# Two placements in a fused attention and long-convolution kernel: the sum of two spectra moved from VectorE to two transfers, and a table's index arithmetic moved behind two copies

## The chip, the cores and the metric

The kernel runs on one core of a Trainium2 chip. The metric is the time of one execution on the device, in microseconds; three runs of the kernel before gave 213.45, 213.49 and 214.47, so the median is 213.49. The engines are TensorE (PE in the profile, with its weight loads as PEld), VectorE (DVE), ScalarE (ACT), GpSimd (POOL) and SyncE (SP). SP, ACT and POOL also issue transfers, each on a queue of its own: q1 is SP's, q10 ACT's, q0 POOL's.

## The reference, cut to what matters

Two independent computations over a sequence of S = 2048 rows of D = 576 columns; their outputs are laid side by side.

```
a:  qkv = x @ wqkv                       # 32 heads of 18
    logits = q . k[s - 2*u], u = 0..7    # sliding window of 8, dilation 2
    attn = softmax(logits); o = sum_u attn * v[s - 2*u]
    a = o @ wo
b:  k_shift = 4-tap causal convolution of k with shift_k
    kv = k_shift * v
    y = causal convolution of kv with ssm_k (length 2048, by FFT) + kv * ssm_D
    b = q * y
out = concatenate([a, b])
```

## The kernel before, in words

**Part b** cuts the sequence into NBL = 4 blocks of BL = 512 rows. Each block of kv ("x" in the names) and each block of the filter is turned into a spectrum by matmuls with tables of sines: `x_spectrum(i)` (L759 to L770, tile `ps_fx`) and `filter_spectrum(m)` (L662). A spectrum has two parts of HB = 4 x 576 = 2304 columns, which ScalarE copies from PSUM to SBUF, x's to the tile `xw`, the filter's to `Ks`. The complex products are made with three multiplications instead of four, and for these each spectrum also needs a third part, the sum of the first two, kept 2 x HB columns behind the first. `XG` gives the place of each x spectrum in `xw`: block 3 has its parts at HB x 6, HB x 7 and HB x 8. HB x 8 is also where block 3 of kv itself lies until its spectrum is made.

Who makes a third part differs. For most, `produce` (L1237) puts an addition on VectorE (L1247) ahead of the first product that needs it. For those listed in the set `given`, `third` (L697) has made it by two transfers earlier: SP copies part 0 to the place of the third part (L700), and POOL adds part 1 to it with an accumulating transfer (`add_half`, L689), which waits for the copy. Before the change this is done for x's block 2 and the filter's block 2 (`third_x(2)`, `third_k(2)`, L1062 and L1063).

Output block j is the sum over i <= j of the products of x's block i with the filter's block j - i. `todo` (L1225) lists the 30 products in the order of (j, t, i), t being one of three thirds of the columns. VectorE makes each (`products`, L1092 to L1100, 128 x 2304 elements), TensorE adds them up in PSUM by matmuls with plus and minus the identity (`sum_of`, L1126, tile `ps_z`), ScalarE evicts the sums to `av` (L1139), TensorE turns them back with the table TI (`inverse`, L1158, tile `ps_inv`; the last piece at L1177) and mirrors them (`ps_back`, L1199 and L1185), ScalarE evicts again, and VectorE multiplies with q ("the gate": L1212 for blocks 0 to 2, L1167 for block 3). `load_q(j)` (L1085) brings the rows of q for this with three transfers on POOL's queue: blocks 0 and 1 ahead of the products, block j + 2 after the gate of block j. `store_b` writes the result.

**Part a** is projections (`ps_proj`), logits (VectorE products at L822, summed by head on TensorE in `ps_log`), a softmax, a weighing of v (VectorE products at L947, summed in `ps_acc`) and the output projection: `output` (L1003) makes one half (288 of 576 columns) of 128 rows of two sequence halves in a PSUM pair `ps_wo`, ScalarE evicts it to a staging tile (L1031), and after the second half ACT issues the store of the tile (L1035). The staging tiles are used in turn: a place in `qk`, one in `TB`, and a second one in `qk` that is dropped once the products of part b have begun. From then on an eviction into a staging tile waits for the store before last.

**Order.** The order of all work is fixed when the program is built. Units of TensorE work stand in one list, `units`; the stages pull them by counts written out by hand (`PLACES`, `FKS`, `FXS`) at calls of `until`, or by `need(label)`, which pulls all units up to the last one with that label. The units of part a's output projection that are left over are interleaved with the products of part b. The loop at the end produces the products up to three ahead of the sums. `ps_wo`, `ps_inv` and most others share two PSUM pairs with tag A, `ps_z` and `ps_acc` two with tag B.

**The start.** The tables are sines of integers. `table` (L419) computes the integers on VectorE into `n_all` with two multiply-adds (L421) and one masking (L422), and returns the function that later has ScalarE take the sines (L423). `table_k(0)` and `table_k(1)` serve the filter's spectra, `table_x(0)` and `table_x(1)` x's. Between them stand two copies of transposed rows of A_x from PSUM into `xT` on VectorE (L510, beside two on ScalarE, L511), which the first projections (`project_first`, L483) read. The list `sines` keeps the four functions in the order table_k(0), table_k(1), table_x(0), table_x(1); ScalarE calls them later in the order 2, 3, 0, 1.

Of the kernel before, what the change touches and what calls it, by code (L numbers as in the profile page):

```python
# [39 lines left out]
def view(t, offset, dims):  # L40

    return bass.AP(tensor=t.tensor, offset=t.offset + offset, ap=[list(t.ap[0])] + [list(d) for d in dims])
# [3 lines left out]
def kernel(  # L46
# [293 lines left out]
    def need(label):  # L340
        while any(u[2] == label for u in units):
            pop()
# [76 lines left out]
    def table(n_i, T, vec, cols, period, offs):  # L419
        for n in range(2):  # L420
            nc.vector.tensor_scalar(n_i[:, n, :], vec, rp[:, cols[n]:cols[n] + 1], offs[n], op0=ALU.mult, op1=ALU.add)  # L421
        nc.vector.tensor_single_scalar(n_i, n_i, period - 1, ALU.bitwise_and)  # L422
        return lambda: nc.scalar.activation(T, n_i, ACT.Sin, bias=pib[:], scale=-2.0 * np.pi / period)  # L423

    def table_k(c):
        return table(n_all[:, 2 * c:2 * c + 2, :], TK[:, c, :, :], n_all[:, 8, :], (2 + c, 2 + c), 2048, (256.0, 1792.0))

    def table_x(n):
        return table(n_all[:, 4 + 2 * n:6 + 2 * n, :], TX[:, 2 * n:2 * n + 2, :], n_all[:, 8, :], (4, 5), 4096,
              (512.0 + 1024.0 * n,) * 2)  # L430
# [31 lines left out]
    def pair_x():  # L462
        return pp.tile([128, 2, 1024], BF16, name="ps_x", tag="B")
# [13 lines left out]
    def project_first(jp, ct0):  # L477

        ps = bank2("ps_proj", "A")
        for e in range(2):  # L480
            c0 = 128 * (ct0 + e)
            for kb in range(4):
                nc.tensor.matmul(ps[:, e, :], wq(kb, 0, c0, 128), xT(kb, 512 * jp, 512), start=(kb == 0), stop=False)  # L483
        for e in range(2):
            nc.tensor.matmul(ps[:, e, :], wq(4, 0, 128 * (ct0 + e), 128)[64 * jp:64 * jp + 64],
                             x5(0)[64 * jp:64 * jp + 64], start=False, stop=True, tile_position=(64 * jp, 0))
        nc.scalar.activation(view(q, S * ct0 + 512 * jp, [[S, 2], [1, 512]]), ps[:], ACT.Copy)

    def spread_taps(n0):
        n = min(256, D - n0)  # L490
        ps = bank2("ps_sk", "A" if n == 256 else "B")
        for h in range(0, n, 128):
            w = min(128, n - h)
            sk = skrow[:, 4 * (n0 + h):4 * (n0 + h + w)].rearrange("p (d j) -> p d j", j=4)
            for r in range(2):
                nc.tensor.matmul(ps[:, h // 128, 0:4 * w], ones96[:, 128 * r:128 * r + 128],  # L496
                                 sk if r else view(skrow, 4 * (n0 + h) + 3, [[4, w], [-1, 4]]),
                                 start=(r == 0), stop=(r == 1))
        nc.scalar.activation(skb[:, :, n0:n0 + n],
                             ps[:].rearrange("p b (d j) -> p j (b d)", j=4)[:, :, 0:n], ACT.Copy)  # L500

    spread_taps(512)
    spread_taps(0)
    sines = [table_k(0), table_k(1)]
    pts = [pair_x() for _ in range(2)]
    for n in range(2):
        transpose_x(0, pts[n], 2 * n, range(4))
# [3 lines left out]
        nc.scalar.activation(xT(2 + n, 0, 512), pts[1][:, n, 0:512], ACT.Copy)  # L511
    copy_tail(0, pts[1])
    spread_taps(256)
    sines += [table_x(0), table_x(1)]
    project_first(0, 0)
    pts = [pair_x() for _ in range(2)]
    for n in range(2):
# [179 lines left out]
    def third(t, at):  # L697

        given.add((t is xw, at))
        nc.sync.dma_start(half(t, at + 2 * HB), half(t, at))  # L700
        add_half(t, at + 2 * HB, at + HB)

    def third_x(i):
        need(f"fx{i}")
        third(xw, HB * XG[i])
# [366 lines left out]
    def upper(t, j, a, width, c0, n):  # L1072

        return bass.AP(tensor=t.tensor, offset=t.offset + (BL * j + 320 - 64 * a) * width + c0,
                       ap=[[width, 64], [(64, 192)[a] * width, 2], [1, n]])
# [9 lines left out]
    def load_q(j):  # L1085
        qB = view(TB, HB * (j % 2), [[D, 4], [1, D]])
        nc.gpsimd.dma_start(qB[:, 0:2], qf[BL * j:BL * j + 256, :].rearrange("(c p) d -> p c d", c=2))  # L1087
        for a in range(2):
            nc.gpsimd.dma_start(qB[64 * a:64 * a + 64, 2:4], upper(qf, j, a, D, 0, D))
        qBs[j] = qB  # L1090
# [134 lines left out]
    todo = [(j, t, i) for j in range(NBL) for t in range(3) for i in range(j + 1)]  # L1225
    load_q(0)
    load_q(1)
    clk["P"] = clk["D"]
    groups = []
    for n, (j, t, i) in enumerate(todo):  # L1230
# [73 lines left out]
```

## Time and profile before

| | us |
|---|---|
| median of three runs | 213.49 |
| the profiled execution, its time | 213.4 |
| the profiled execution, its span | 211.7 |
| TensorE busy in the span | 200.2 |
| VectorE busy | 197.5 |
| ScalarE busy | 150.7 |
| GpSimd busy | 71.5 |

The profile is of one execution. All times within it count from the start of the span; the time of an execution is somewhat longer than the span, here by 1.7 us. A row of a timeline gives the start, the duration of the merged instructions, the engine, the line of the kernel, the operation, "out<-in" with the tiles' names, the shape, the count, and in brackets the idle time of the engine just before and what ended it. A row of the table by stretches gives, for each engine, the busy time within the stretch and the count of instructions, and after them the granted TensorE clock (1.00 is full), the mean busy share of the 16 DMA engines, and what they moved in GB/s. A row of DMA issues gives the tiles, the issuing engine, the count, the size of one, and the median time from issue to landing; a row of a DMA queue gives its packets, the MB moved, and the time of its packets as a share of 16 engines over the stretch asked for.

### The profile page before, as it was taken

To read this page: it belongs to the slowest core of one execution; us is meant where nothing else is said; L and a number is where in the kernel's file an instruction comes from. 1 tells how busy PE (TensorE), PEld (TensorE's weight loads), DVE (VectorE), ACT (ScalarE), POOL (GpSimd) and SP (SyncE) were. 2 spreads that over 40 slices of the span, in tenths; PEclk is the share of its full clock that TensorE was granted. 3 is DMA by queue.
4 is the path that set the end of the run, shared out by engine and by line. 5 is a ranking of instruction groups with operands and counts; after the bars stand their busy time and mean duration, and the time that the engine had idled before them with its cause. 6 is when DMAs were issued, how large, how long until landed. Compare 5 with 4: busy or idle time off the path is not lost.

```text
span 211.7 us, 5087 instructions
## 1 busy us (share of the span) xinstructions
PE 200.2 (95%) x2114; PEld 113.1 (53%) x2122; DVE 197.5 (93%) x150; ACT 150.7 (71%) x218; POOL 71.5 (34%) x104
## 2 busy tenths in 40 slices
PE   7999899999879999999999999999999999999891
PEld 3543344444545556563345556765566667676560
DVE  7999999999978999979979999999999999899982
ACT  3699766967796989984378678864487897765640
POOL 8999995021591467220090000004240000302000
PEclk9999999999999999999999999999999999999999
DMA  6999999999193636999999797598993105453034
GB/s 205 302 337 225 267 329 301 189 282 190 35 127 41 87 54 102 186 160 181 228 241 225 133 220 167 101 211 249 209 278 109 60 3 158 124 167 115 3 105 118
DMA packets 34084, 36.12 MB, mean 171 GB/s; under 512 B 17459, under 2 KB 28847, under 8 KB 34062
## 3 DMA queue, kind: packets, MB, share of 16 engines
q1 hardware_dynamic: 26380, 23.11, 44.2%
q0 software_dynamic: 5216, 10.19, 24.7%
q10 hardware_dynamic: 2466, 2.51, 3.6%
q8 instruction: 16, 0.26, 0.5%
q14 instruction: 6, 0.05, 0.1%
HBM read 13.11 MB, written 4.72 MB: 84 GB/s over the span
## 4 chain that ended last, share of the span: by engine, by line
PE 83%; ACT 10%; issue 3%; DVE 2%; DVEq 0%; ACTq 0%
PE ps_proj L363 15%; PE ps_z L1126 9%; PE ps_wo L1020 8%; PE ps_acc L964 7%; PE ps_inv L1158 7%; PE ps_fx L766 7%; PE ps_log L837 4%; PE ps_proj L483 3%; PE ps_fk L610 3%; ACT Ks L670 3%; PE ps_proj L374 3%; PE ps_proj L367 3%; PE ps_rev L650 1%; PE ps_sk L496 1%; ACT qk L397 1%
## 5 line engine op out<-in xcount | busy, mean ns | idle before, releaser
L363 PE MATMUL ps_proj<-xw 128*128 128x512 bf16 x153 | 36.2, 380 | 1.3 <-issue 0.6
L822 DVE TENSOR_TENSOR av<-qk 128x4096 bf16<-128x4096 bf16 (+1 forms) x16 | 31.5, 2018 | 2.3 <-ACT xw L592 2.3
L363 PEld LDWEIGHTS <-xw 128*128 128x128 bf16 x160 | 14.4, 98 | 20.0 <-issue 4.9
L1139 ACT ACTIVATE av<-ps_z 128x768 bf16<-128x768 f32 x23 | 17.4, 809 | 5.5 <-PE ps_z L1126 5.5
L768 ACT ACTIVATE xw<-ps_fx 128x576 bf16<-128x576 f32 x32 | 18.8, 670 | 2.4 <-PE ps_fx L766 2.4
L397 ACT ACTIVATE qk<-ps_proj 128x1024 bf16<-128x1024 f32 x14 | 14.3, 1023 | 8.3 <-PE ps_proj L374 4.7
L670 ACT ACTIVATE Ks<-ps_fk 128x576 bf16<-128x576 f32 x32 | 18.9, 683 | 1.1 <-PE ps_fk L611 1.0
L1098 DVE TENSOR_TENSOR qk<-xw,Ks 128x2304 bf16<-128x2304 bf16 x14 | 18.6, 1354 | 1.0 <-PE ps_z L1126 0.7
L560 DVE TENSOR_TENSOR tB<-kj,skb 128x4608 bf16<-128x4608 bf16 (+1 forms) x8 | 19.4, 2431 | 0.1
L766 PE MATMUL ps_fx<-xw,TB 128*128 128x288 bf16 x128 | 17.9, 286 | 0.8 <-ACT xw L592 0.7
L1020 PE MATMUL ps_wo<-qk 128*128 128x288 bf16 x128 | 18.0, 287 | 0.0
L610 PE MATMUL ps_fk<-Ks,TB 128*128 128x384 bf16 x62 | 16.4, 326 | 1.2 <-ACT Ks L670 0.9
L1158 PE MATMUL ps_inv<-av,TI 128*128 128x288 bf16 (+1 forms) x112 | 15.6, 292 | 0.6 <-ACT av L1139 0.6
L766 PEld LDWEIGHTS <-TB 128*128 128x128 bf16 x128 | 12.0, 98 | 6.7 <-issue 3.5
L1087 POOL DMA_DIRECT2D TB<-in_B_q_dram x4 | 2.9, 736 | 36.7 <-DVE v L1098 23.6
L964 PE MATMUL ps_acc<-av,ident 64*64 64x512 bf16 x160 | 15.3, 379 | 0.0
L611 PE MATMUL ps_fk<-Ks,TB 128*128 128x192 bf16 x62 | 15.2, 246 | 0.0
L397 ACT ACTIVATE v<-ps_proj 128x1024 bf16<-128x1024 f32 x9 | 9.3, 1040 | 7.8 <-PE ps_proj L363 4.3
L1020 PEld LDWEIGHTS <-qk 128*128 128x128 bf16 x128 | 11.5, 98 | 6.3 <-issue 3.6
L968 ACT ACTIVATE qk<-ps_acc 128x1024 bf16<-128x1024 f32 x8 | 8.2, 1024 | 8.3 <-PE ps_acc L964 8.3
L947 DVE TENSOR_TENSOR av<-Ks,v 128x4096 bf16<-128x4096 bf16 x6 | 13.6, 2286 | 0.1
L1158 PEld LDWEIGHTS <-TI 128*128 128x128 bf16 x112 | 10.5, 98 | 5.6 <-issue 2.7
(194 smaller groups left out, 468.2 us busy)
## 6 DMA issues: line engine op xcount, KB each, us to landing
Ks<-Ks POOLq DMA_DIRECT2D x7, 576.0 KB, 8.5
TB<-av SPq DMA_DIRECT2D x12, 256.0 KB, 5.5
kj<-in_B_k_dram SPq DMA_DIRECT2D x6, 504.0 KB, 5.8
vt<-in_B_v_dram SPq DMA_DIRECT2D x8, 288.0 KB, 4.9
Ks<-av SPq DMA_DIRECT2D x8, 256.0 KB, 5.7
out_dram<-qk ACTq DMA_DIRECT2D x5, 288.0 KB, 3.2
Ks<-in_A_x_dram SPq DMA_DIRECT2D x2, 576.0 KB, 5.1
xw<-in_A_wqkv_dram SPq DMA_DIRECT2D x2, 576.0 KB, 5.8
```

The lines of the kernel that those rows point to most:

```text
L363: nc.tensor.matmul(ps[:, jp, :], wq(kb, comp, 128 * ct, 128), xT(kb, 1024 * jj + 512 * jp, 512), **se)
L397: nc.scalar.activation(view(t, o + pad + 1024 * jj, [[512, 2], [1, 512]]), ps[:], ACT.Copy)
L560: dve(2304 * n, lambda: nc.vector.tensor_tensor(to, view(kj, row * D, [[D, n], [D, 4], [1, D]]), view(skb, row * D, [[D, n], [0, 4], [1, D ...
L610: nc.tensor.matmul(o[:, 0:2], w, rhs[:, 0:2], start=start, stop=stop)
L670: nc.scalar.activation(view(Ks, k_at(m, cs ^ (m & 1)) + 96 * gi, [[768, 3], [384, 2], [1, 96]]), acc3(ps), ACT.Copy, scale=(PSG, MSG)[cs][ ...
L766: nc.tensor.matmul(ps[:, pm, 0:HD], TX[:, 2 * pm + c, 128 * gi:128 * gi + 128], kv[:, 2 * c + pm, HD * h:HD * h + HD], start=(c == 0), sto ...
L768: nc.scalar.activation(view(xw, HB * XG[i] + 96 * gi + 1152 * h, [[HB, 2], [384, 3], [1, 96]]), view(ps, 0, [[512, 2], [96, 3], [1, 96]]), ...
L822: return P, at, step, dve(1024 * nj, lambda: nc.vector.tensor_tensor(view(P, at, [[step, 4], [256, nj], [1, 256]]), view(t, o + 256 * hh, ...
L964: nc.tensor.matmul(acc[64 * o:64 * o + 64, h, :], ident[64 * h:64 * h + 64, 64 * h:64 * h + 64], view(P, 256 * u, [[2048, 2], [1, 256]])[6 ...
L1020: nc.tensor.matmul(ps[:, r, 0:HD], oT(hh, j + 2 * r, t)[:, o:o + 128], wo[:, t // 2, t % 2, HD * h:HD * h + HD], start=(t == 0 and h == 0) ...
L1126: nc.tensor.matmul(view(acc[r], 512 * h, [[192, 2], [96, 2], [1, 96]])[o:o + 64], w[64 * h:64 * h + 64, 64 * h:64 * h + 64], pr[64 * h:64 ...
L1158: nc.tensor.matmul(ps[:, c, 0:n], TI[:, sl, pm, 128 * c:128 * c + 128], Yall[:, j % 2, pm, sl, c0:c0 + n], start=(pm == 0 and sl == 0), st ...
```

## The change

Three edits, two of which belong together:

```diff
     spread_taps(512)
     spread_taps(0)
-    sines = [table_k(0), table_k(1)]
+    sines = [table_k(0)]
     pts = [pair_x() for _ in range(2)]
...
     copy_tail(0, pts[1])
     spread_taps(256)
-    sines += [table_x(0), table_x(1)]
+    sines += [table_k(1), table_x(0), table_x(1)]
     project_first(0, 0)
...
     load_q(0)
     load_q(1)
+    third_x(3)
     clk["P"] = clk["D"]
```

The first two move the index arithmetic of `table_k(1)` on VectorE from ahead of the two copies of L510 to behind them. The order of the four functions in `sines` stays, and with it the order on ScalarE.

The third lists block 3 of x in `given`, so `produce` no longer puts VectorE's addition of 128 x 2304 elements ahead of the product (j, t, i) = (3, 0, 3). In its place `third` issues two transfers of 128 x 2304 elements within `xw`: a plain one on SP's queue, behind the third part of the filter's block 2, and an adding one on POOL's queue, behind the six transfers of q for blocks 0 and 1. The functions that it calls are as they were:

```python
    def add_half(t, to, of):
        nc.gpsimd.dma_start(half(t, to), half(t, of), accum_op=ALU.add, max_dma_last_dim=HB)
...
    def third(t, at):
        given.add((t is xw, at))
        nc.sync.dma_start(half(t, at + 2 * HB), half(t, at))
        add_half(t, at + 2 * HB, at + HB)
...
    def third_x(i):
        need(f"fx{i}")
        third(xw, HB * XG[i])
```

The order of the instructions on TensorE and ScalarE is the same in both kernels. VectorE has one instruction less and the two copies earlier; SP and POOL have one transfer more each.

## Prediction
> **What bounds the kernel now.** I read the page's totals and chain first, then the table of busy time by stretches for the end, then timelines of single engines around the two places that the change touches, and last the DMA views around the new transfers.
>
> ```profile
> span 211.7 us, 5087 instructions
> PE 200.2 (95%) x2114; PEld 113.1 (53%) x2122; DVE 197.5 (93%) x150; ACT 150.7 (71%) x218; POOL 71.5 (34%) x104
> ...
> PE 83%; ACT 10%; issue 3%; DVE 2%; DVEq 0%; ACTq 0%
> ...
> 185.00:190.00 5.00, 5.00 (x73) 3.48 (x72) 5.00 (x5) 2.72 (x5) 0.00 (x0) 1.00 0.52 168
> 190.00:195.00 5.00, 5.00 (x88) 3.27 (x90) 4.90 (x5) 2.91 (x5) 1.92 (x3) 1.00 0.42 130
> ```
>
> TensorE and VectorE are both nearly always busy, and the totals do not say which one sets the end. The chain does: 83% of it is TensorE, 2% VectorE. In the end stage (columns: stretch, its length, then busy time of PE, PEld, DVE, ACT and POOL, granted clock, DMA share, GB/s) both are full from 185 to 195, TensorE at full clock. What matters is which of them waits for the other there.
>
> ```profile
> 189.18 1.35 DVE L1247 TENSOR_TENSOR xw<-xw 128x2304 bf16<-128x2304 bf16 x1
> 190.63 1.36 DVE L1098 TENSOR_TENSOR qk<-xw,Ks 128x2304 bf16<-128x2304 bf16 x1
> 194.44 2.62 DVE L1098 TENSOR_TENSOR qk<-xw,Ks 128x2304 bf16<-128x2304 bf16 x2
> 202.06 1.35 DVE L1212 TENSOR_TENSOR TB<-v,TB 128x2304 bf16<-128x2304 bf16 x1
> 204.31 0.96 DVE L1137 CAST av<-ps_z 128x768 bf16<-128x768 f32 x1 [0.90 <-PE ps_z L1126]
> ...
> 197.13 0.35 PE L1126 MATMUL ps_z<-qk,ident 64*64 64x384 bf16 x4
> ...
> 198.55 1.46 PE L1158 MATMUL ps_inv<-av,TI 128*128 128x384 bf16 x8 [0.58 <-ACT av L1139]
> ```
>
> VectorE's last products end at 202.06 (it starts the gate there) and it then stands 0.90 us until TensorE has made the sum that it casts. TensorE's only sizeable gap, 0.58 us, is ScalarE's eviction of a sum that TensorE itself had just finished. So at the end TensorE leads and VectorE follows.
>
> **The change part by part.** *The removed VectorE addition.* It is the row at 189.18; the next instruction starts at 190.63, so 1.45 us of VectorE time go. The products behind it come up to 1.45 us earlier. The tightest of them is the second of the pair at 194.44: it ends at 194.44 + 2.62 = 197.06, and TensorE takes it up at 197.13, 0.07 us later, with no idle time printed before it. All that follows on VectorE ends in the wait of 0.90 us, which becomes about 2.35. I put the gain at 0. The bounds are 0 and 1.45 us, the latter if TensorE were in truth waiting at 197.13. The cover is TensorE's own row of work; with that gone, the whole 1.45 would be gained.
>
> *The table's index arithmetic.*
>
> ```profile
> 5.09 1.80 PE L450 MATMUL ps_x<-ident,Ks 128*128 128x128 bf16 x16
> 5.66 0.93 DVE L421 TENSOR_SCALAR Ks<-Ks,rp 128x512 int32<-128x512 int32 x2
> 7.16 1.04 PE L496 MATMUL ps_sk<-tB,ones 97*128 97x512 bf16 x4
> 7.24 0.75 DVE L510 COPY xw<-ps_x 128x512 bf16<-128x512 bf16 x2
> 8.03 1.89 PE L483 MATMUL ps_proj<-xw 128*128 128x512 bf16 x8
> 11.56 1.36 DVE L560 TENSOR_TENSOR xw<-kj,skb 128x2304 bf16<-128x2304 bf16 x1 [0.42 <-ACT qk L487]
> ```
>
> The two copies move ahead of one table (three instructions, 5.66 to 7.24). Their source, the first eight transposes, is there at about 5.09 + 1.80/2 = 6.0, so they start about 1.2 us earlier. TensorE reads them in L483 at 8.03, but it is busy with L496 from 7.16 until then: gain 0. VectorE would stand for about 6.0 - 5.7 = 0.3 us ahead of the copies, and the last table ends that much later; the 0.42 us idle ahead of L560 take it. Without that cover it would cost 0.3 us. I take 0, bounds -0.1 to +0.3.
>
> *The two new transfers.* The plain one goes on SP behind the third of Ks (SP row at 142.41 below) and needs only the last spectrum's evictions, which are over by then, so it starts near 143. The adding one goes on POOL behind the six transfers of q, the last of them issued by 154.82 + 1.24 = 156.06, and takes some 1.2 us to issue: traffic from about 157.5. Behind it on POOL stand only the next rows of q at 179.61. SP's next issue is at 176.80. So neither queue is held up. Its reader, the product at 190.63, comes some 25 us after any landing seen (at most 8.5 us); that wait costs nothing.
>
> ```profile
> 142.41 0.52 SPq L700 DMA_DIRECT2D Ks<-Ks  x1
> ...
> 176.80 0.42 SPq L1080 DMA_DIRECT2D out_dram<-TB  x1
> ...
> 146.19 1.18 POOL L689 DMA_DIRECT2D Ks<-Ks  x1 [0.75 <-issue]
> ...
> 154.82 1.24 POOL L1089 DMA_DIRECT2D TB<-in_B_q_dram  x2
> 179.61 0.73 POOL L1087 DMA_DIRECT2D TB<-in_B_q_dram  x1 [23.55 <-DVE v L1098]
> ...
> Ks<-Ks POOLq DMA_DIRECT2D x1, 576.0 KB, 8.5
> ```
>
> What they do cost is room on the DMA engines, and there one transfer is already waited for:
>
> ```profile
> 157.56 0.38 ACTq L1035 DMA_DIRECT2D out_dram<-qk  x1
> ...
> 162.08 0.65 ACT L1031 ACTIVATE qk<-ps_wo 128x576 bf16<-128x576 f32 x1 [1.44 <-DMA out_dram<-qk]
> 162.62 1.51 ACT L1139 ACTIVATE av<-ps_z 128x768 bf16<-128x768 f32 x2
> ...
> out_dram<-qk ACTq DMA_DIRECT2D x1, 288.0 KB, 4.4
> ...
> 161.75 2.17 PE L1020 MATMUL ps_wo<-qk 128*128 128x288 bf16 x16
> 163.99 0.33 PE L1126 MATMUL ps_z<-qk,identn 64*64 64x384 bf16 x4
> ```
>
> The store issued at 157.56 lands 4.4 us later, at 161.96, and ScalarE, which fills the same staging rows again, stands 1.44 us for it until 162.08. Behind that eviction on ScalarE's queue are the two evictions of sums at 162.62. TensorE's next output unit, the second half of the row at 161.75 (from about 162.84), needs the PSUM pair that the waiting eviction frees at 162.08 + 0.65 = 162.73. The slack is 0.1 us: any later landing goes nearly whole into TensorE, and there is no later gap that takes it back. So the price of the change is how much later this store lands.
>
> ```profile
> 147.61 0.38 ACTq L1035 DMA_DIRECT2D out_dram<-TB  x1
> ...
> out_dram<-TB ACTq DMA_DIRECT2D x1, 288.0 KB, 7.2
> ...
> 160.66 0.38 ACTq L1035 DMA_DIRECT2D out_dram<-TB  x1
> ...
> out_dram<-TB ACTq DMA_DIRECT2D x1, 288.0 KB, 2.2
> ...
> q0 software_dynamic: 234, 0.50, 86.8%
> q10 hardware_dynamic: 147, 0.17, 18.3%
> ...
> q10 hardware_dynamic: 255, 0.28, 30.6%
> ...
> 156.00:158.00 2.00, 2.00 (x26) 1.44 (x28) 1.90 (x4) 1.53 (x3) 0.06 (x1) 1.00 1.02 265
> 158.00:160.00 2.00, 2.00 (x31) 1.40 (x24) 1.91 (x3) 1.96 (x4) 0.00 (x0) 1.00 0.75 219
> 160.00:162.00 2.00, 2.00 (x33) 1.22 (x32) 2.00 (x2) 0.64 (x2) 0.00 (x0) 1.00 0.26 90
> ```
>
> A store of the same size landed in 2.2 us with the engines free (issued at 160.66), in 4.4 us beside the tail of q, and in 7.2 us where two adding transfers were under way (issued at 147.61). The rows of q0 and q10 with 86.8% and 18.3% are of 148.8 to 152.0, beside those adds; 30.6% is q10 in 157.5 to 160.2, nearly all of the store in question. In the former, the adds moved 0.50 MB in 0.868 x 3.2 = 2.78 us of all engines, so 0.59 MB of one add need some 3.3 us. The DMA share is 1.02 until 158 and falls after it, and into that fall the add is put: its 3.3 us lie right beside the store. The plain copy lands its own load on an interval (143 to 147) from which the engines are full up to 158, and so pushes the rows of q back by its size, bounded by 0 and by the cost of an add, 3.3 us.
>
> Bounds for the store's landing: 4.4 us (no effect) and 7.2 us (wholly beside adds), with some delay of q's tail on top, at most 9. As its first microsecond still runs beside q as before and the rest beside the add, I take two thirds of the way from 4.4 to 7.2, or 6.3 us: landing at 163.9, 1.9 us later, less 0.1 us slack is 1.8 us. The second store (160.66) is then late too, but the eviction that waits for it stands on ScalarE's queue behind the delayed ones and moves with them. Sum: 0 + 0 + 1.8. The profiled execution took 213.4 us (span 211.7 and 1.7 around it; the median of the runs is 213.49): 213.4 + 1.8 = 215.2 us.
>
> **The rivals.** *The store takes turns evenly with the add.* From the rows above a packet of an add takes 0.868 x 3.2 x 16 / 234 = 0.19 us on its engine, one of a store 0.183 x 3.2 x 16 / 147 = 0.064 us; a store has 255/16 = 16 for each engine. Alone they need 1.0 of the 2.2 us, so 1.2 us are fixed. One for one with the add: 1.2 + 16 x 0.254 = 5.3 us, a landing 0.9 us later, +0.8: 214.2 us. Against it: in 148.8 to 152.0 there went 234 packets of the add to 147 of the store, 1.6 to one, at which the store takes 1.2 + 16 x 3.2 / (147/16) = 6.8 us, or +2.3 (215.7). The Trainium skill ("DMA: Bandwidth & Descriptors", section "Queues, rings and completion order") states the even turn, each DMA engine going round its queue rows packet by packet; by that rule the sum would be 214.2, and the trace agrees only in part, with 1.6 to one.
>
> *The transfers are hidden anyway.* If POOL issues the add later than I count, or the store's data is through before the add's begins, nothing moves: 213.4. For it: the DMA share is down to 0.26 from 160 on, so most of the store's bytes had gone by then. Against: a share of 1.02 just before.
>
> *Faster: VectorE did set TensorE's pace.* The 0.07 us at 197.13 say that the product arrived just in time; if the weight loads ahead of it had been held back, TensorE's stretch from 190 on would shrink with VectorE. It decides from the point at which a product is later than TensorE's own readiness, and gives at most 1.45: 212.0, likelier half of it, 212.7. Against it stand 5.00 us of TensorE in each of the two stretches from 185 to 195, and the first gap after them waits for ScalarE.
>
> *Worse: both adverse bounds meet*, q pushed back and the store starved until the add is done, landing 8.7 us after issue: 166.3, +4.1, 217.5.
>
> **How the numbers follow.** Forecast case (delay of 1.1 to 3 us) 0.47; the worse case 0.08; even turns 0.22; hidden 0.13; faster 0.10. Own range of the forecast: 214.5 to 216.4. A measurement of this kernel tells about 0.5% (1.07 us) from no change. Slower by more: 0.47 + 0.08 = 0.55. Even turns, hidden and the smaller half of the faster case lie within it: about 0.38. Faster by over 0.5%: 0.07. The range leaves out the upper part of the worse case and the full gain: 213.0 to 217.0.
>
> **What would show it.** ScalarE's wait for the store ahead of L1031 at 162.08 should grow from 1.44 to about 3.3 us, the store's landing from 4.4 to about 6.3, and an idle stretch of about 1.8 us should appear on TensorE ahead of an L1020 near 162.8. The adding transfer should issue near 156 and land before 168. From 190 on VectorE should wait longer for TensorE, the 0.90 us ahead of the cast growing to some 2.3. At the start L483 should still begin at 8.0 and L560 at 11.6. I am wrong if the landing stays below 5 us (no change), if the end stage from 185 to the end shrinks by over 0.5 us (VectorE led), or if a wait for the added transfer shows up ahead of the product that reads it.

## The result and the profile after

| | before | after |
|---|---|---|
| median, us | 213.47 (213.36 to 214.47, 4 runs) | 220.63 (218.37 to 221.70, 4 runs) |
| the profiled execution, its time | 213.4 | 221.7 |
| its span | 211.7 | 220.0 |

The ratio of the times is 1.0293, 95% interval 1.0243 to 1.0344: the change makes the kernel about 6 us slower. The ratio leaves out executions that took over 1.5% longer than the fastest of the same kernel, here the profiled one of the changed kernel, while the medians are of all. The place is the one that the prediction named, the size is not. The timeline of ScalarE in the kernel after, with the stores that ACT issues:

```profile
159.06 0.38 ACTq L1035 DMA_DIRECT2D out_dram<-qk  x1
...
168.65 0.65 ACT L1031 ACTIVATE qk<-ps_wo 128x576 bf16<-128x576 f32 x1 [6.50 <-DMA out_dram<-qk]
```

The same wait was 1.44 us before. TensorE's timeline behind it:

```profile
163.26 1.15 PE L1020 MATMUL ps_wo<-qk 128*128 128x288 bf16 x8
169.35 1.94 PE L1020 MATMUL ps_wo<-qk 128*128 128x288 bf16 x8 [4.93 <-ACT qk L1031]
...
173.59 2.13 PE L1158 MATMUL ps_inv<-av,TI 128*128 128x288 bf16 x16
```

Before, both output units stood in one row without a gap (161.75, 2.17 us for 16), and the inverse followed 2.56 us after the start of the second (162.84):

```profile
165.40 2.13 PE L1158 MATMUL ps_inv<-av,TI 128*128 128x288 bf16 x16
```

Now 4.93 us lie between them, and the second, the same eight matmuls, takes 1.94 us in place of 1.15. The table by stretches says why (the last three columns are the granted clock, the DMA share and GB/s):

```profile
170.00:171.00 1.00, 1.00 (x6) 0.49 (x4) 0.00 (x0) 1.00 (x2) 0.00 (x0) 0.50 0.00 0
...
172.00:173.00 1.00, 1.00 (x16) 0.54 (x12) 0.00 (x0) 0.41 (x1) 0.00 (x0) 0.53 0.88 308
173.00:174.00 1.00, 1.00 (x20) 0.56 (x13) 0.98 (x1) 0.61 (x1) 0.00 (x0) 1.00 0.01 3
```

After the idle stretch TensorE runs at half clock, from 169.5 to 172.9. The store's landing, from the table of DMA issues, and the packets of the two queues in the stretches 157.5 to 159.5, 159.5 to 162, 162 to 165 and 165 to 168.6 (where q10 is left out it has no row: it moved nothing):

```profile
out_dram<-qk ACTq DMA_DIRECT2D x1, 288.0 KB, 9.5
...
q0 software_dynamic: 145, 0.52, 99.7%
q10 hardware_dynamic: 51, 0.05, 10.2%
...
q0 software_dynamic: 152, 0.50, 95.5%
...
q0 software_dynamic: 243, 0.58, 98.0%
q10 hardware_dynamic: 53, 0.06, 7.1%
...
q10 hardware_dynamic: 485, 0.52, 42.3%
q0 software_dynamic: 78, 0.14, 21.2%
```

The 51 packets of q10 in the first stretch are of the store before. The store in question, issued at 159.06, gets no packet through until 163.8, 4.7 us later, while POOL's queue moves 0.97 MB. From then on the two queues take turns, three packets for four; the row of 164 to 165:

```profile
q0 software_dynamic: 69, 0.16, 83.5%
q10 hardware_dynamic: 51, 0.06, 20.4%
```

So most of the store's delay lies ahead of its first packet: about 3.9 of the 5.1 us, since in the kernel before the first packet came 0.85 us after issue. The traces do not show what holds that packet back. The adding transfer was issued where the prediction had it, 1.5 us later like all around it:

```profile
157.54 1.31 POOL L689 DMA_DIRECT2D xw<-xw  x1
```

The sum for the profiled execution, by starts of the same instructions in both kernels: the first output unit starts at 163.26 against 161.75 (+1.5, from an earlier wait of which more below); from it to the second 169.35 - 163.26 = 6.09 against 1.09, half of 2.17 (+5.0); from there to the inverse at L1158 173.59 - 169.35 = 4.24 against 165.40 - 162.84 = 2.56 (+1.7, the half clock); from there to the end 46.4 against 46.3 (+0.1). Together +8.3, the difference of the spans. This execution is the slowest of four; the median is lower.

The removed addition shows up in VectorE's timeline as waiting, not as time:

```profile
199.95 1.36 DVE L1098 TENSOR_TENSOR av<-xw,Ks 128x2304 bf16<-128x2304 bf16 x1 [1.22 <-PE ps_z L1126]
...
212.50 0.96 DVE L1137 CAST av<-ps_z 128x768 bf16<-128x768 f32 x1 [1.04 <-PE ps_z L1126]
```

A new wait of 1.22 us for TensorE and 0.14 us more ahead of the cast make 1.36 of the 1.45 us that went. Kernels 7, 8 and 10 below, where the addition is gone too, show the same pair of waits (1.22 or 1.23 and 1.04 or 1.05).

### The profile page after: what moved, and what is told of

Read it like the earlier page. It is cut to its first block, busy times and chain, and to the rows that moved or that the text cites. A ratio compares the mean times of both kernels' runs of the same rounds, so it can differ in the third digit from the quotient of the medians.

```text
span 220.0 us, 5102 instructions
## 1 busy us (share of the span) xinstructions
PE 202.3 (92%) x2122; PEld 113.3 (51%) x2122; DVE 196.6 (89%) x149; ACT 151.0 (69%) x218; POOL 72.8 (33%) x105
## 4 chain that ended last, share of the span: by engine, by line
PE 70%; DMA 11%; ACT 8%; SPq 4%; issue 3%; DVE 2%; POOL 0%; DVEq 0%; ACTq 0%
PE ps_proj L363 13%; PE ps_z L1126 8%; PE ps_inv L1158 7%; PE ps_acc L964 7%; PE ps_fx L766 6%; PE ps_wo L1020 5%; DMA out_dram<-qk 4%; SPq L212 3%; PE ps_proj L483 3%; PE ps_log L837 3%; DMA Ks<-in_B_ssm_k_dram 3%; DMA Ks<-Ks 3%; PE ps_fk L610 3%; PE ps_proj L374 2%; ACT Ks L670 2%
## 5 line engine op out<-in xcount | busy, mean ns | idle before, releaser
L363 PE MATMUL ps_proj<-xw 128*128 128x512 bf16 x160 | 37.5, 380 | 0.5 <-ACT qk L397 0.5
L1020 PE MATMUL ps_wo<-qk 128*128 128x288 bf16 x128 | 18.9, 295 | 4.9 <-ACT qk L1031 4.9
L560 DVE TENSOR_TENSOR tB<-kj,skb 128x4608 bf16<-128x4608 bf16 (+1 forms) x8 | 19.4, 2429 | 0.1
L1020 PEld LDWEIGHTS <-qk 128*128 128x128 bf16 x128 | 11.7, 100 | 11.6 <-issue 8.7
L1158 PE MATMUL ps_inv<-av,TI 128*128 128x288 bf16 (+1 forms) x112 | 15.6, 292 | 0.6 <-ACT av L1139 0.6
L1158 PEld LDWEIGHTS <-TI 128*128 128x128 bf16 x112 | 10.5, 98 | 5.6 <-issue 2.7
```

The costliest lines, as they stand in the source:

```text
L363: nc.tensor.matmul(ps[:, jp, :], wq(kb, comp, 128 * ct, 128), xT(kb, 1024 * jj + 512 * jp, 512), **se)
L560: dve(2304 * n, lambda: nc.vector.tensor_tensor(to, view(kj, row * D, [[D, n], [D, 4], [1, D]]), view(skb, row * D, [[D, n], [0, 4], [1, D ...
L1020: nc.tensor.matmul(ps[:, r, 0:HD], oT(hh, j + 2 * r, t)[:, o:o + 128], wo[:, t // 2, t % 2, HD * h:HD * h + HD], start=(t == 0 and h == 0) ...
L1158: nc.tensor.matmul(ps[:, c, 0:n], TI[:, sl, pm, 128 * c:128 * c + 128], Yall[:, j % 2, pm, sl, c0:c0 + n], start=(pm == 0 and sl == 0), st ...
```

## The experiments

Ratios are to the kernel before, run beside each on the same chip (its median was 213.47 to 213.72), with 95% intervals. "Store" is the time from issue to landing of the store near 157.6, "idle" TensorE's gap ahead of the second output unit, "half clock" what follows that gap, all from the one profiled execution of each kernel. Without any added transfer near it the store landed after 3.8 to 5.3 us (before, 2, 7, 9 and 10), so a landing up to 5.3 us shows no effect by itself.

| kernel | store, us | idle, us | half clock | span, us | median, us | ratio |
|---|---|---|---|---|---|---|
| before | 4.4 | 0 | no | 211.7 | 213.47 | 1 |
| changed | 9.5 | 4.93 | yes | 220.0 | 220.63 | 1.0293 (1.0243 to 1.0344) |
| 1: transfers only | 8.0 | 3.41 | yes | 217.8 | 219.64 | 1.0280 (1.0221 to 1.0340) |
| 2: table only | 5.3 | 0.8 | no | 212.8 | 213.24 | 0.9993 (0.9966 to 1.0020) |
| 3: plain copy only | 5.1 | 0.55 | no | 212.6 | 215.04 | 1.0066 (1.0041 to 1.0091) |
| 4: adding transfer only | 6.8 | 2.19 | yes | 215.8 | 217.96 | 1.0164 (1.0102 to 1.0225) |
| 5: transfers and VectorE's addition | - | - | - | - | 219.85 | 1.0271 (1.0235 to 1.0307) |
| 6: add ahead of q | 8.1 | 3.5 | yes | 218.7 | 219.88 | 1.0295 (1.0270 to 1.0320) |
| 7: transfers late | 3.8 | 0 | no | 216.7 | 213.75 | 1.0012 (0.9977 to 1.0048) |
| 8: third staging place | 8.6 | 0 | no | 212.5 | 214.78 | 1.0037 (1.0007 to 1.0067) |
| 9: before, third place | 4.0 | 0 | no | 211.4 | 213.17 | 0.9983 (0.9960 to 1.0005) |
| 10: late, third place, table | 4.3 | 0 | no | 211.7 | 213.78 | 1.0007 (0.9981 to 1.0034) |
| 11: add in small pieces | 7.9 | 3.37 | yes | 216.4 | 218.23 | 1.0196 (1.0146 to 1.0247) |
| 12: half an add only | 5.3 | 0.75 | no | 212.9 | 214.44 | 1.0028 (0.9993 to 1.0063) |

The theory (S): the store is held up behind POOL's queue, ScalarE stands for it, and TensorE stands for ScalarE and then runs at half clock. The rivals: the moved table costs part of it (T); the removed addition was on the path and pays some back (V).

**1, the transfers alone, and 2, the table alone.**

```diff
 kernel 1, against before
     load_q(1)
+    third_x(3)
 kernel 2, against before
-    sines = [table_k(0), table_k(1)]
+    sines = [table_k(0)]
...
-    sines += [table_x(0), table_x(1)]
+    sines += [table_k(1), table_x(0), table_x(1)]
```

> Only the two transfers in place of VectorE's addition; the table's arithmetic stays where it was. Theory S (the store issued by ACT near 157.6 is starved by POOL's queue, TensorE stands for it and then runs at half clock): ScalarE's wait ahead of the eviction L1031 near 162 is 5 to 7 us, TensorE idle 4 to 5.5 us ahead of an L1020, then some 3.4 us at a granted clock of 0.5; time 218 to 220. Theory T (the moved table costs the part of the loss that lies at 60 to 67 us of the span): the wait of TensorE for a transfer into Ks ahead of L650 (2.1 us in the changed kernel) is gone, and this kernel is some 1.9 us faster than the changed one. If the wait is there as well, T falls.

> Only the table's arithmetic behind the copies; VectorE's addition stays. Theory S: 213.4 within 0.5 us, as the store's wait is as before (1.4 us). Theory T: about 215.3, with the wait ahead of L650 of some 2 us. If neither, the wait ahead of L650 comes and goes from run to run.

TensorE's timeline of kernel 1:

```profile
161.60 1.16 PE L1020 MATMUL ps_wo<-qk 128*128 128x288 bf16 x8
166.16 2.08 PE L1020 MATMUL ps_wo<-qk 128*128 128x288 bf16 x8 [3.41 <-ACT qk L1031]
...
171.12 2.48 PE L1158 MATMUL ps_inv<-av,TI 128*128 128x288 bf16 x16
```

The transfers alone make the whole loss; its profile has the idle stretch and the half clock and no wait ahead of L650. Its span by the same differences: 161.60 against 161.75 (-0.15), 4.56 against 1.09 (+3.5), 4.96 against 2.56 (+2.4), 46.7 against 46.3 (+0.4), together +6.1. Of the last 0.4 us, 0.35 is the half clock, which reaches into the inverse (2.48 us for 2.13). The idle stretch was shorter than expected (3.4 us, not 4 to 5.5). The table alone changes nothing that can be measured, so T falls. The profiled execution of kernel 2 is its second slowest of twelve, and its store and its idle stretch in the table are longer than in the kernel before, without any added transfer. The wait ahead of L650 comes from elsewhere, and no edit decides it: kernels 6 and 7 have it with the table in its old place, and kernel 10 does not have it with the table moved. The rows of TensorE's timeline for the changed kernel, kernel 2 and kernel 7, one fence each:

```profile
67.38 0.41 PE L650 MATMUL ps_rev<-Ks,flip2r 128*128 128x288 bf16 x2 [2.14 <-DMA Ks<-Ks]
```

```profile
66.13 0.41 PE L650 MATMUL ps_rev<-Ks,flip2r 128*128 128x288 bf16 x2 [0.76 <-DMA Ks<-Ks]
```

```profile
68.73 0.41 PE L650 MATMUL ps_rev<-Ks,flip2r 128*128 128x288 bf16 x2 [3.26 <-DMA Ks<-Ks]
```

It is absent in the kernel before and in the profiles of kernels 1, 3 and 8 to 12. It goes with the time at which SP's three transposing loads of the filter at L212 are over. They take 8.51 us in the kernel before and 11.78 in the changed one (rows of SP's timeline):

```profile
40.95 8.51 SPq L212 DMA_TRANSPOSE Ks<-in_B_ssm_k_dram  x3
```

```profile
41.39 11.78 SPq L212 DMA_TRANSPOSE Ks<-in_B_ssm_k_dram  x3
```

Over the profiles of this case there is no wait where they are over by 52.2, none or 0.48 us at 52.4 (kernels 9 and 4), 0.76 at 52.6, 1.80 and 2.14 at 53.2 (kernel 6 and the changed one), and 3.26 at 54.0. Why those loads differ between executions was not tried.

**3, the plain copy alone, 4, the adding transfer alone, and 12, half of it.** VectorE's addition is kept in all three and writes the right sums over the place afterwards.

```diff
     load_q(1)
+    nc.sync.dma_start(half(xw, HB * XG[3] + 2 * HB), half(xw, HB * XG[3]))      # kernel 3
+    add_half(xw, HB * XG[3] + 2 * HB, HB * XG[3] + HB)                          # kernel 4
+    nc.gpsimd.dma_start(view(xw, HB * 8, [[1, HB // 2]]), view(xw, HB * 7, [[1, HB // 2]]),
+                        accum_op=ALU.add, max_dma_last_dim=HB)                  # kernel 12
```

> Only the plain transfer is added; VectorE's addition writes the third part over it. If the copy's load pushes the rows of q back and the store with them, the store near 157.6 lands 5.5 to 6.5 us after issue and the time is 214.5 to 215.5. If the adding transfer alone starves the store, it lands within 5 us and the time is 213.5.

> Only the adding transfer is added, behind the rows of q, without the copy ahead of it; VectorE's addition writes the third part over it. If the add alone starves the store: landing 7.5 to 9 us after issue, ScalarE's wait 4.5 to 6 us, time 217 to 219. If it takes the copy to push the rows of q back into the store: landing 5 to 6.5 us, time 214 to 215.5.

> Only an adding transfer of half the size (half of the columns), no copy; VectorE's addition writes all of the third part over it. With the whole one the store landed 6.8 us after issue, TensorE stood 2.2 us and then ran some 3.5 us at half clock. Theory S: landing 5.5 to 6 us, ScalarE's wait 2.4 to 3.0 us, TensorE idle 0.8 to 1.5 us. If that little idle time also brings the half clock, the time is 216 to 217; if not, 214.3 to 215.3.

TensorE's timelines of kernels 3, 4 and 12:

```profile
163.57 1.14 PE L1020 MATMUL ps_wo<-qk 128*128 128x288 bf16 x8 [0.55 <-ACT qk L1031]
```

```profile
165.30 2.08 PE L1020 MATMUL ps_wo<-qk 128*128 128x288 bf16 x8 [2.19 <-ACT qk L1031]
...
169.50 2.13 PE L1158 MATMUL ps_inv<-av,TI 128*128 128x288 bf16 x16
```

```profile
164.05 1.14 PE L1020 MATMUL ps_wo<-qk 128*128 128x288 bf16 x8 [0.75 <-ACT qk L1031]
```

By the ratios each transfer costs something by itself, the copy 0.7% and the add 1.6%, together 2.3% against 2.8% for both in kernel 1, whose interval begins at 2.2%. The add delays the store directly (6.8 us, a little under what was expected). The copy's part does not show in the landing of kernel 3, whose profiled execution is the fastest of its twelve: 5.1 us is within what kernel 2 had without any transfer. What the copy does show is that it pushes back the work on POOL's queue: the adding transfer of the filter, ahead of q, landed 8.4 to 8.8 us after issue in every profile read here without the copy and 9.4 to 10.0 in every one with it (the row is of kernel 3):

```profile
Ks<-Ks POOLq DMA_DIRECT2D x1, 576.0 KB, 9.4
```

That this is how the copy reaches the store is likely, but argued. The three timelines also show the second step: after 0.55 and 0.75 us of idle time the eight matmuls take 1.14 us as ever, after 2.19 us they take 2.08. From that unit to L1158 kernel 4 needs 4.20 us against 2.56, so 2.2 us of idle time cost 3.8. Kernel 12 came out at the low end of what was expected, with an interval that reaches no change.

**11, the add in small pieces, and 6, the add ahead of q.**

```diff
 kernel 11, against before
     load_q(1)
+    given.add((True, HB * XG[3]))
+    nc.sync.dma_start(half(xw, HB * 8), half(xw, HB * 6))
+    nc.gpsimd.dma_start(half(xw, HB * 8), half(xw, HB * 7), accum_op=ALU.add, max_dma_last_dim=D)
 kernel 6, against before
+    third_x(3)
     load_q(0)
     load_q(1)
```

> The two transfers at the changed kernel's place, but the adding one in pieces of 288 elements (576 bytes) instead of 1152. If POOL's queue takes turns with ACT's piece by piece, smaller pieces leave the store a larger share: its landing falls from 8.0 to 5 to 6.5 us and the time to 215 to 217. If the store simply stands behind what POOL has issued before it, it lands as late or later (8 us or more, the adding transfer being slower in small pieces), and the time is 219 to 222.

> The same two transfers, but the adding one on POOL's queue ahead of the rows of q, so that it runs near 149 to 157 and the rows of q stand beside the store near 157.6. If what starves the store is the amount of work on POOL's queue ahead of or beside it, whichever transfer that is: ScalarE's wait 4 to 7 us and 217.5 to 220. If it is the adding transfer itself (rows of q leave the store its turn): wait 2 to 3 us and 214.5 to 215.5.

Packets of kernel 11 in 160 to 162 and 162 to 164, and of kernel 1 in the same two stretches (q10 has no row in its first):

```profile
q0 software_dynamic: 405, 0.28, 96.1%
q10 hardware_dynamic: 101, 0.12, 20.2%
...
q0 software_dynamic: 452, 0.26, 96.5%
q10 hardware_dynamic: 172, 0.18, 32.3%
```

```profile
q0 software_dynamic: 179, 0.41, 107.9%
...
q10 hardware_dynamic: 341, 0.38, 55.8%
q0 software_dynamic: 94, 0.19, 50.4%
```

In small pieces the add lets ACT's queue in earlier (first packet 3.4 us after issue, 4.6 in kernel 1), but it moves fewer bytes itself (0.28 and 0.26 MB against 0.41) and lasts longer, and the store lands as late, 7.9 us after issue. The time fell between the two expectations. Ahead of q the loss is the same as behind it: whichever of POOL's transfers stands beside the store, q or the add, holds it up, so the kind of that transfer is not what matters. In kernel 6 ACT's queue did get packets all along (395 to POOL's 510 from 157 to 165), but they were in part those of the store before, issued at 154.08, which itself landed only after 10.8 us. So there the store was slowed behind a backlog of both queues. That the amount of work in this stretch is what counts is likely: half the add (kernel 12) delayed the store less than the whole (kernel 4), 5.3 us against 6.8, though 5.3 is no more than kernel 2 had without any.

**5, the transfers and VectorE's addition too, and 7, the transfers held back.**

```diff
 kernel 5, against before
     load_q(1)
+    nc.sync.dma_start(half(xw, HB * XG[3] + 2 * HB), half(xw, HB * XG[3]))
+    add_half(xw, HB * XG[3] + 2 * HB, HB * XG[3] + HB)
 kernel 7, against before
-    given = set()
+    given, cell = set(), main.tile([1, 1], BF16, name="cell")
...
             prs[n] = products(*todo[n])
+            if n == 8:
+                nc.sync.dma_start(cell[:], prs[n][0][0:1, 0, 0:1])
+                third_x(3)
```

> Both transfers as in the change, and VectorE's addition kept behind them (it waits for the adding transfer's landing and writes the same sums); the table stays. Against the kernel with the transfers alone (219.64) this puts back 1.45 us of VectorE work. Theory S (VectorE follows TensorE at the end, its addition is worth nothing): the same time, 218.5 to 220.5. Theory V (the addition was on the path and its removal pays back part of the loss): 1 to 1.5 us slower, 220.7 to 221.

> The same two transfers, but held back until the ninth product is made (about 169 us of the span): SP first moves one element of that product to a cell, then issues the copy, and POOL adds behind it. Nothing waits for a store there. Theory S: ScalarE's wait near 162 is back at 1.4 us, no low clock, and the time is that of the kernel before, 213.0 to 214.0, as the removed addition is worth nothing. Theory V: 212.0 to 212.7.

Putting the addition back costs nothing that shows (219.85 against 219.64), and taking it away without the collision gains nothing (213.75, ratio 0.9977 to 1.0048, where V wanted 212.7 or less): V falls from both sides, the second of which is the firmer. The profiled execution of kernel 5 took 334 us at a mean granted clock of 0.56 and is used for nothing here; without it the median is 219.43. In kernel 7 the adding transfer issues at 178.3, and the store is undisturbed. Its profiled execution is its slowest (218.38); the span is long by the 3.26 us ahead of L650 and a half clock behind them.

**8, a third staging place for the output projection, 9, the same in the kernel before, and 10, all harmless parts together.**

```diff
-    av = sv.tile([128, 6 * 2048], BF16, name="av")
+    av = sv.tile([128, 6 * 2048 + 384], BF16, name="av")
...
             if homes_st[-1][1] == 13312 and npr[0]:
-                homes_st.pop()
-                homes_st.rotate(-1)
+                homes_st[-1] = (av, 11520)
```

This is all of kernel 9 against before. Kernel 8 has `third_x(3)` behind `load_q(1)` as well, as kernel 1 has. Kernel 10 has this, the edits of kernel 7 and the moved table.

> The two transfers at the changed kernel's place, and a third staging place (in av, made 384 columns wider) for the output projection instead of two, so that the eviction near 162 no longer waits for the store near 157.6 but fills another place. Theory S: the store still lands 7 to 10 us after issue, but nothing stands for it until about 165; the loss is mostly gone, 213.3 to 215. If the load of the transfers itself slowed the engines, or something else of the change did, the time stays at 217 to 220.

> The kernel before with the third staging place in av in place of two, no other edit. Theory S: ScalarE's wait of 1.4 us near 162 goes, but TensorE did not stand for it, so the time is the same, 213.0 to 213.8. If the median falls below 213.0, the store's wait cost TensorE something in some executions of the kernel before too.

> All that was found harmless together: the transfers held back until the ninth product, the third staging place, and the table's arithmetic behind the copies. Theory S: 212.8 to 213.8, no better than the kernel before by more than 0.3 us. If it is over 0.5 us faster, the parts that do nothing one by one do something together.

ScalarE's timeline of kernel 8:

```profile
161.26 0.65 ACT L1031 ACTIVATE av<-ps_wo 128x576 bf16<-128x576 f32 x1 [0.51 <-PE ps_wo L1012]
...
166.39 0.65 ACT L1031 ACTIVATE qk<-ps_wo 128x576 bf16<-128x576 f32 x1 [2.53 <-DMA out_dram<-qk]
```

The store still lands late (8.6 us), but the eviction that freed TensorE's PSUM now goes to `av` at 161.26 without waiting for it. The wait moves to the next use of the place in `qk`, at 166.39, where TensorE hardly needs it (a gap of 0.45 us). With the same two transfers in the same place, 2.8% of loss become 0.4% (0.1% to 0.7%). This is the step that shows the cause: both transfers run where they did and the store is as late, only the waiter is gone. Kernels 9 and 10 are no different from the kernel before within their intervals; kernel 9 has the lowest median of all (213.17), but its interval reaches 1.0005, so no version here is shown to beat the kernel before.

## Why the prediction was right or wrong

*VectorE's addition is worth 0*: right. Kernel 7 shows it and kernel 5 agrees, and the 1.36 us of new waiting ahead of two of its instructions is where the time went. That all of it would gather ahead of the cast was wrong; most came earlier, at 199.95.

*The table's arithmetic is worth 0*: right for the time (0.9993). Two details were off. L483 and L560 did not stay at 8.0 and 11.6: in the changed kernel they start at 7.58 and 11.80. And the cover by L496 depends on when x lands. In the profiled execution of kernel 1, with the table in its old place, L496 was over earlier and TensorE did stand 0.43 us for the copies; with the table moved it did not. Nothing of it reaches the end.

*Both queues are free for the transfers, and the product that reads the third part never waits*: right; no wait for the added transfer is in any profile. It was not "at most 8.5 us" to its landing, though, but 10.8 in the changed kernel; that figure was one row, and adding transfers in the kernel before took up to 11.9.

*The store near 157.6 lands later, ScalarE stands for it, and TensorE behind ScalarE with 0.1 us of slack*: right in every link. The extra landing time of 0.7, 0.9, 2.4, 3.6 and 5.1 us (kernels 3, 12, 4, 1 and the changed one, against 4.4) became 0.55, 0.75, 2.19, 3.41 and 4.93 us of idle time on TensorE, so the slack was 0.15 to 0.2 us. Kernel 8 cuts the link, and all but 0.4% of the loss goes.

*The store lands 6.3 us after issue, so the price is 1.8 us*: this is the step that failed. The landing measured 8.0 us with the transfers alone and 9.5 in the changed kernel, so the term is 3.5 to 5.0 us. The size came from reading the row of 148.8 to 152.0, beside two adds, as one even state and taking two thirds of the way to the landing of that store, 7.2 us. It is two states. The store there, issued at 147.61, has no packet through until 149.5; after that the queues go one for one. Rows of 147.6 to 149.5 and of 150 to 152.5 in the kernel before:

```profile
q0 software_dynamic: 158, 0.33, 103.0%
...
q0 software_dynamic: 168, 0.38, 83.2%
q10 hardware_dynamic: 163, 0.19, 25.9%
```

So what grows with the work ahead is the time to the first packet: 0.8 to 0.9 us with the engines free (the store issued at 175.05), 1.9 us here, 4.6 in kernel 1 and 4.7 in the changed one, where the copy's load, q and the add lay ahead in one go. In kernel 4 single packets come from 2.2 us on, but only 14 to POOL's 120 between 160.0 and 161.4. The sum had no such term. The case called worse (8.7 us, by its own figures +4.2 and not +4.1) came near the delay and was given 0.08, but it too lacked the half clock. The rival of 214.2 priced even turns rightly (0.254 us a pair on an engine; 2.5 x 16 / 163 = 0.245 here) and missed the same time ahead of them, so its size did not come. The Trainium skill ("DMA: Bandwidth & Descriptors", section "Queues, rings and completion order") lets each DMA engine go round its queues packet by packet; the trace agrees once the store's packets have begun (168 to 163) and does not show it in the time before.

*A missing term*: the sum took an idle stretch of TensorE at its own length. In fact the idle stretches of 2.19 to 4.93 us here all brought half clock, for 1.5 us more in kernel 11, 1.6 to 1.7 in kernels 4, 6 and the changed one, and 2.8 in kernel 1. How long the idle stretch is does not decide it alone: 2.14 us ahead of L650 in the changed kernel and 1.80 there in kernel 6 brought none. The row behind the former, with the granted clock third from the end, and in kernel 1 the rows in which the half clock begins, with TensorE still idle, and ends:

```profile
67.00:68.00 1.00, 0.62 (x6) 0.49 (x6) 0.26 (x1) 0.00 (x0) 0.00 (x0) 1.00 0.63 79
...
165.00:166.00 1.00, 0.00 (x0) 0.00 (x0) 1.00 (x2) 0.54 (x1) 0.00 (x0) 0.51 0.16 56
...
171.00:172.00 1.00, 1.00 (x9) 0.60 (x6) 1.00 (x2) 1.00 (x2) 0.00 (x0) 0.57 0.03 8
```

The half clock lasted 3.4 us in the changed kernel and in kernels 4, 6 and 11, and 6.8 us, twice that, in kernel 1, the first 1.1 of them with TensorE still idle. This is most of what kernel 1 lost more than kernel 11 in the profiles (spans 217.8 and 216.4) at the same idle time. The Trainium skill ("TensorE: Matmul & The Clock Gate", section "Part 1: The HAM clock gate") says that TensorE drops to half clock after an idle window of about 3.4 us and needs about 3.4 us of work to come back. The trace agrees on the way back in the changed kernel (169.5 to 172.9), less so in kernel 1 (5.7 us of work, 166.16 to 171.85), and shows the drop after as little as 2.19 us in kernel 4. The kernel before could not show it: behind its first two microseconds its idle stretches are at most 0.73 us, and its granted clock stays at 1.00.

With both terms the profile of kernel 1 adds up: 213.4 - 0.15 + 3.5 + 2.4 + 0.4 = 219.5 against the 219.56 that this execution took. This is an account after the fact. The +1.5 ahead of the first output unit in the changed kernel's profile is the wait ahead of L650, which no edit here decides.

## What to carry to other kernels

When a change adds transfers, look for the transfer that some engine already stands for, follow the waiter to the bounding engine, and price the delay by all the work that is queued at that moment, not by the best similar row. Cut such a row into short stretches first: a mean share can hide a time without any packet and a time of even turns. A small wait that costs nothing (here 1.44 us with 0.1 us of slack behind it) is a fuse: check what the next microsecond there costs before loading the same resource. And once the added idle time of TensorE comes near 2 us, count the half clock after it as well, as a chance at that length and as a term from there on.

## What the runs showed of the hardware

A store on ACT's queue got no packet through for 4.7 us while transfers issued earlier on POOL's queue filled the engines (159.06 to 163.8 in the changed kernel), and one issued with the engines free for 0.8 to 0.9 us (at 175.05 in the kernel before). After that the two queues took turns nearly one for one (163 to 168 from 150 to 152.5 in the kernel before), but not at once in kernel 4 (14 to 120 from 160.0 to 161.4). Cutting the add into pieces of 576 bytes brought the first packet forward, to 3.4 us, but not the landing (7.9 us against 8.0). TensorE's granted clock fell to 0.50 with idle stretches of 2.19 us and more near the store and stayed at 1.00 with 2.14, 1.80 and 0.75 us; in kernels 1 and 4 it fell 2.3 and 2.1 us after the idle stretch began, in the changed kernel only 5.1 us after, when work had already resumed. The half clock lasted 3.4 us, or twice that. The same three transposing loads of the filter took 8.51 us in one execution and 11.78 in another; there the first output unit then came 1.5 us later.
